# Masking the second batch's scores on TensorE inside the first layer, and moving two batches' global queries to the next first layer

## The chip, the cores and the metric

The kernel runs on one core of a Trainium2 chip. The metric is the time of one execution on the device, in microseconds (us). Lower is better. Most executions of one kernel agree within some 0.3%. A run more than 1.5% above the fastest of its kernel is called slow and is left out of every comparison. In a profile, PE is TensorE (matmuls), PEld its weight loads, DVE is VectorE, ACT is ScalarE, POOL is GpSimd and SP is SyncE, whose queue issues nearly all transfers. The granted clock is TensorE's clock as the profile records it, as a share of full speed.

## The reference

The program is an attention, followed by two dense layers with a gate between them. There are 8 batches of 8 heads with 512 local and 32 global tokens of width 64. A local query sees all global keys and the local keys within 32 positions. A global query sees everything.

```python
s_g   = scale * q_g @ concat(k_g, k_l).T;  out_g = softmax(s_g) @ concat(v_g, v_l)
s_ll  = where(abs(i - j) <= 32, scale * q_l @ k_l.T, -1e9)
s_lg  = scale * q_l @ k_g.T
out_l = softmax(concat(s_lg, s_ll)) @ concat(v_g, v_l)
x = concat(out_g, out_l) as (4608 tokens, 512)
h = x @ w_in                        # 512 x 2048
y = (h * clip(h + 3, 0, 6) / 6) @ w_out   # 2048 x 512
```

## The kernel before

The heads are worked in pairs. There are four pairs to a batch, so 32 in all, and pairs 0 to 3 are the first batch. A pair goes through these steps:

- load q, k and v, and cast them to fp16;
- transpose q and k (`emit_T` on TensorE, `emit_TD` by DMA from pair 8 on);
- score in two blocks of 128x512 for each head, with the exponential on ScalarE and the window mask;
- multiply with V and normalise (`emit_AV`), then transpose the output (`emit_X`).

The global queries have their own scores (`emit_SG`) and their own product with V (`emit_PG`). That product reads a V tile in which the last 63 columns of each head hold ones, so that the sums of the softmax come out of the same matmul. The texts below call these columns "the ones". The dense layers of a batch are cut into units: 16 of the first layer (`u1`, four 128x512 matmuls each) and 16 of the second (four each). `M(n)` issues the next n units that wait in a list. From the third batch on these units are woven between the attention steps of the next batch.

The mask is made in two ways. The first batch adds minus 30000 on TensorE, by an identity matmul that opens the group. All later batches multiply by 0 or 1 on VectorE:

```python
def emit_S(p, ch, pe_mask=False):
    ...
    if pe_mask:
        for e in range(2):
            nc.tensor.matmul(out=pss[e], lhsT=ident, rhs=mneg[:, ch], start=True, stop=False, ...)
    for w in range(NT): ...            # eight score matmuls of 128 columns
    for e in range(2):
        nc.scalar.activation(out=E[:, ch, e], in_=pss[e], func=EXP, scale=qk_scale)
    for e in range(0 if pe_mask else 2):
        nc.vector.tensor_tensor(out=E[:, ch, e], in0=E[:, ch, e], in1=mk[:, ch]..., op=mult)
```

`pin` fixes the program order of some engines. The GpSimd and SP queues are pinned everywhere, all five engines at the start, and only TensorE besides the queues in the second batch. The part at issue, after the first batch's attention:

```python
u1(HEAD)
nc.vector.tensor_scalar(out=mk..., in0=mneg, ...)       # 0/1 mask
for c in range(HEAD + 1, HEAD + 6):
    u1(c)
emit_G(1, 4, "kg")          # cast and transpose global keys of batches 2 to 4
u1(HEAD + 6)
emit_G(0, 4, "qg")          # the same for global queries
u1(HEAD + 7)
...
emit_SG(0) ... emit_PG(3)   # global queries of batch 1
pin(*ALL)
for p in range(NM, NPAIR):  # pairs 4 to 31
    load(p + 5); ...
    if p == 2 * NM - 1:     # the last pair of batch 2: first layer of batch 2 follows
        ...
    pin(*QUEUES, *((ET.PE,) if b == 1 else ()))
```

The softmax here doesn't subtract the row's maximum and nothing guards it: scores larger than these inputs give would overflow.

## Time and profile before

| | before |
|---|---|
| median time (beside the changed kernel) | 339.94 us, 339.4 to 341.44 in 4 runs |
| span of the profiled run | 337.2 us |
| TensorE busy, mean granted clock | 313.1 us (93%), 0.953 |
| VectorE, ScalarE, GpSimd busy | 229.0, 198.8, 133.1 us |

A high busy share of TensorE doesn't mean useful work at full speed. Matmuls at half clock also count as busy, so busy time has to be read together with the clock: from 57.1 to 71.9 us the clock was 0.50, and TensorE still counts as busy for 9.45 of 14.80 us. The prediction quotes the views by stage. One row of the costliest groups is needed besides (line, engine, operation, output and inputs, number, then busy us, mean ns of one, and idle time before them with what ended it):

```profile
L257 DVE TENSOR_TENSOR E<-E,mk 128x512 f16<-128x512 f16 x108 | 59.9, 586 | 22.0 <-ACT E L254 20.2
```

These are 108 of the mask multiplies. Four more are on another line, so there are 112: seven batches of 16.

### The profile page before, as it was taken

To read this page: it belongs to the slowest core of one execution; us is meant where nothing else is said; L and a number is where in the kernel's file an instruction comes from. 1 tells how busy PE (TensorE), PEld (TensorE's weight loads), DVE (VectorE), ACT (ScalarE), POOL (GpSimd) and SP (SyncE) were. 2 spreads that over 40 slices of the span, in tenths; PEclk is the share of its full clock that TensorE was granted. 3 is DMA by queue.
4 is the path that set the end of the run, shared out by engine and by line. 5 is a ranking of instruction groups with operands and counts; after the bars stand their busy time and mean duration, and the time that the engine had idled before them with its cause. 6 is when DMAs were issued, how large, how long until landed. Compare 5 with 4: busy or idle time off the path is not lost.

```text
span 337.2 us, 7418 instructions
## 1 busy us (share of the span) xinstructions
PE 313.1 (93%) x2784; PEld 165.2 (49%) x2784; DVE 229.0 (68%) x499; ACT 198.8 (59%) x394; POOL 133.1 (39%) x224
## 2 busy tenths in 40 slices
PE   6897794579999999999999999999999999999994
PEld 2453353444555555555555555555555555444571
DVE  7578688767946578847995689479945892473170
ACT  3588295637833459645974597458745881372260
POOL 7999999357203363326433633264230000000000
PEclk9699698569999999999999999999999999999999
DMA  8999999996099999769898997798943003101102
GB/s 215 316 362 271 331 361 209 187 200 126 2 171 193 204 204 175 144 129 217 167 149 167 206 178 134 130 231 172 136 124 99 18 16 80 62 0 33 71 24 62
DMA packets 139571, 52.92 MB, mean 157 GB/s; under 512 B 126992, under 2 KB 131088, under 8 KB 139536
## 3 DMA queue, kind: packets, MB, share of 16 engines
q1 hardware_dynamic: 137360, 52.19, 71.0%
q0 software_dynamic: 2176, 0.26, 1.2%
q8 instruction: 22, 0.36, 0.5%
q14 instruction: 13, 0.11, 0.1%
HBM read 35.13 MB, written 8.91 MB: 131 GB/s over the span
## 4 chain that ended last, share of the span: by engine, by line
PE 83%; DVE 5%; ACT 4%; POOL 3%; DMA 2%; issue 1%; POOLq 0%
PE po L397 35%; PE psH L381 33%; PE psS L250 4%; DVE gt L388 2%; PE pav L318 2%; PE pav L315 2%; DMA stg<-in_k_g_dram 2%; PE pg L338 2%; ACT vt L472 1%; PE psSG L292 1%; ACT t L386 1%; PE psS L269 1%; DVE xn L324 1%; PE psX L354 1%; DVE E L257 1%
## 5 line engine op out<-in xcount | busy, mean ns | idle before, releaser
L397 PE MATMUL po<-wout,gt 128*128 128x512 f16 x544 | 125.5, 379 | 0.0
L381 PE MATMUL psH<-xt,win 128*128 128x512 f16 x512 | 120.3, 385 | 0.5 <-DVE xt L358 0.5
L388 DVE SCALAR_TENSOR_TENSOR gt<-t,psH 128x512 f16<-128x512 f32 (+1 forms) x144 | 92.0, 654 | 27.5 <-ACT t L386 27.1
L386 ACT ACTIVATE t<-psH,half_col 128x512 f32<-128x512 f32 (+1 forms) x144 | 93.0, 669 | 26.7 <-PE psH L381 26.0
L254 ACT ACTIVATE E<-psS 128x512 f16<-128x512 f32 x108 | 55.6, 603 | 54.6 <-PE psS L250 54.6
L381 PEld LDWEIGHTS <-win 128*128 128x128 f16 x576 | 54.2, 99 | 55.1 <-issue 3.4
L397 PEld LDWEIGHTS <-gt 128*128 128x128 f16 x544 | 49.9, 98 | 54.3
L257 DVE TENSOR_TENSOR E<-E,mk 128x512 f16<-128x512 f16 x108 | 59.9, 586 | 22.0 <-ACT E L254 20.2
L238 POOL COPY qT<-qT 128x32 f16<-128x32 f16 x24 | 5.2, 216 | 119.0 <-DMA qT<-qn 93.4
L401 ACT COPY ot<-po 128x512 f32<-128x512 f32 x17 | 10.0, 586 | 29.4 <-PE po L397 29.4
L324 DVE TENSOR_TENSOR xn<-pav,rc 128x256 f16<-128x256 f32 x64 | 26.0, 420 | 1.3
L401 DVE COPY ot<-po 128x512 f32<-128x512 f32 x17 | 11.7, 691 | 19.4 <-PE po L397 19.4
L136 POOL CAST vt<-stg 128x512 f16<-128x512 f32 x32 | 21.5, 673 | 1.5 <-DMA stg<-in_v_l_dram 1.3
L315 PE MATMUL pav<-vt,E 128*128 128x65 f16 x256 | 21.2, 197 | 0.9 <-ACT E L254 0.9
L318 PE MATMUL pav<-vb,E 128*128 128x65 f16 x256 | 21.2, 198 | 0.0
L141 POOL COPY vb<-vt 64x512 f16<-64x512 f16 x32 | 20.1, 627 | 2.1
L323 DVE RECIPROCAL rc<-pav 128x4 f32<-128x4 f32 x64 | 10.1, 172 | 15.5 <-PE pav L318 15.4
L136 POOL CAST qn<-stg 128x512 f16<-128x512 f32 x31 | 20.5, 662 | 0.0
L315 PEld LDWEIGHTS <-E 128*128 128x128 f16 x256 | 18.9, 101 | 3.1
L318 PEld LDWEIGHTS <-E 128*128 128x128 f16 x256 | 17.9, 100 | 3.8 <-issue 1.0
L136 POOL CAST kn<-stg 128x512 f16<-128x512 f32 x31 | 19.4, 625 | 0.9
L250 PE MATMUL psS<-qT,kT 64*128 64x128 f16 x432 | 17.8, 224 | 1.5 <-DVE qT L222 1.5
(83 smaller groups left out, 261.8 us busy)
## 6 DMA issues: line engine op xcount, KB each, us to landing
stg<-in_k_l_dram SPq DMA_DIRECT2D x32, 256.0 KB, 3.8
stg<-in_q_l_dram SPq DMA_DIRECT2D x32, 256.0 KB, 4.2
stg<-in_v_l_dram SPq DMA_DIRECT2D x32, 256.0 KB, 4.7
out_dram<-ot SPq DMA_DIRECT2D x24, 256.0 KB, 2.3
stg<-in_moe_w_in_dram SPq DMA_DIRECT2D x16, 256.0 KB, 5.7
stg<-in_moe_w_out_dram SPq DMA_DIRECT2D x16, 256.0 KB, 5.7
out_dram<-ot SPq DMA_DIRECT2D x8, 192.0 KB, 2.2
out_dram<-ot SPq DMA_DIRECT2D x16, 64.0 KB, 1.8
```

Source lines behind the costliest of these rows:

```text
L136: eng.tensor_copy(out=o, in_=s[c + "f"])
L250: nc.tensor.matmul(out=pss[2 * ch + e][:, w * P:(w + 1) * P], lhsT=kT[r, c0:c0 + P], rhs=qT[r, w * P:(w + 1) * P])
L254: nc.scalar.activation(out=E[:, ch, e], in_=pss[2 * ch + e], func=EXP, scale=qk_scale)
L257: nc.vector.tensor_tensor(out=E[:, ch, e], in0=E[:, ch, e], in1=mk[:, ch].rearrange("p w c -> p (w c)"), op=mult)
L315: nc.tensor.matmul(out=o, lhsT=E[:, 0, e, w * P:(w + 1) * P], rhs=vt[:, w, h, 0:D + 1], start=True, stop=False, skip_group_check=True)
L318: nc.tensor.matmul(out=o, lhsT=E[:, 1, e, w * P:(w + 1) * P], rhs=vb[:, (w - 1) % NT, h, 0:D + 1], start=False, stop=True, skip_group_chec ...
L324: nc.vector.tensor_tensor(out=xn[:, 2 * w2:2 * w2 + 2].rearrange("p w (e d) -> p w e d", e=2), in0=pv[:, :, :, 0:D], in1=rc.to_broadcast([ ...
L381: nc.tensor.matmul(out=ps[:, 0:n], lhsT=w_in_t[m][:, c * P:(c + 1) * P], rhs=rhs(m), start=(m == 0), stop=(m == NM - 1), skip_group_check= ...
L386: nc.scalar.activation(out=t1[:, 0:n], in_=ps[:, 0:n], func=RELU, bias=half_col, scale=1.0 / 6.0)
L388: nc.vector.scalar_tensor_tensor(out=gts[c][:, 0:n], in0=t1[:, 0:n], scalar=1.0, in1=ps[:, 0:n], op0=amin, op1=mult)
L397: nc.tensor.matmul(out=po[t][:, 0:dm], lhsT=gts[c][:, t * P:(t + 1) * P], rhs=w_out_t[c // 4][:, c % 4], start=(c == 0), stop=(c == NC - 1))
L401: (nc.scalar.copy if t % 2 else nc.vector.tensor_copy)(out=ot, in_=po[t][:, 0:dm])
```

## The change

The intent is to give TensorE work to do while the second batch's attention waits for the other engines. The first layer of batch 1 is woven with that attention instead of running ahead of it. Batch 2's masks go to TensorE, where there is room, because VectorE would otherwise be too full. The global queries of batches 1 and 2 move into the first layer of batch 2. The order of all engines is now fixed up to the scores of pair 8. Besides this, pair 1 is loaded and cast earlier, the casts of global keys and queries are issued ahead of their transposes, and half of the fills of ones go from ScalarE to VectorE.

```diff
     load(0, "kq")
     load_g(0, 1, "kg")
+    load(1, "kq")
     load(0, "v")
-    for p in range(1, NM):
+    load(1, "v")
+    for p in range(2, NM):
         load(p, "kqv")
@@ first layer of batch 1, cut
-    for c in range(HEAD + 1, HEAD + 6):
-        u1(c)
-    emit_G(1, 4, "kg")
-    u1(HEAD + 6)
-    emit_G(0, 4, "qg")
+    u1(3)
+    u1(4)
+    cast_G(1, 4, "kg")
+    u1(5)
+    u1(6)
+    emit_G(1, 4, "kg")
+    ...
+    emit_T(5, True)
+    u1(9)
+    emit_S(4, 0)           # emit_S now always masks on TensorE
+    u1(10)
+    emit_S(4, 1)
+    ...                    # pairs 5 to 7 in the same way, up to u1(15)
+    emit_AV(7)
+    M(1)
+    emit_X(7)
+    M(2)
+    po_end = units.pop(0)
+    ...
+    emit_G(0, 4, "qg")
+    M(2)
+    po_end()               # first output tile of batch 1, and its stores
+    emit_SG(0)
+    ...
+    for p in range(NM):
+        emit_PG(p)
+    emit_XG(0)
+    feed(4)                # loads, casts, DMA transposes for later pairs
+    M(1)
+    emit_SG(4)
+    ...
+    for u in range(NT):
+        ones_v(1, u, nc.vector)     # was on ScalarE, in the first stage
+    M(2)
+    feed(5)
+    for p in range(NM, 2 * NM):
+        emit_PG(p)
+    emit_XG(1)
+    ...
+    pin(*ALL)
+    emit_S2(2 * NM)
@@ in the loop, now from pair 8 on
-        if p == 5:
+        if p == 9:
             load_g(4, B, "kg"); load_g(4, B, "qg")
```

More of the change, by code (lines that the diff above doesn't have):

```diff
@@ L145, in vglob, with vgsum @@
                         in_=vg[rg, b].unsqueeze(1).to_broadcast([Sg, NT, H, D]))
-        if b:
-            eng.tensor_copy(out=vgs[b % NV][rg, :, 0:D], in_=vg[rg, b])
+    def vgsum(b, eng):
+        eng.tensor_copy(out=vgs[b % NV][rg, :, 0:D], in_=vg[rg, b])
     def load_vg(b):
@@ L181, in load_g, with cast_G @@
         gst[b0, nm] = t
+    def cast_G(b0, b1, nm):
+        n = wrk.tile([P, 4 * P], FP16, tag="gn", name=nm + "n", bufs=2)
+        nb = b1 - b0
+        nc.vector.tensor_copy(out=n[:, 0:nb * P], in_=gst[b0, nm][:, 0:nb * P])
+        gst[b0, nm, "n"] = n
     def emit_G(b0, b1, nm):
         nb = b1 - b0
-        n = wrk.tile([P, 4 * P], FP16, tag="gn", name=nm + "n", bufs=2)
-        nc.vector.tensor_copy(out=n[:, 0:nb * P], in_=gst[b0, nm][:, 0:nb * P])
+        if (b0, nm, "n") not in gst:
+            cast_G(b0, b1, nm)
+        n = gst[b0, nm, "n"]
         psT = ps_tile("psGT", FP16)
@@ L258, in emit_S2, with emit_Sm, emit_Ss @@
                                         in1=mk[:, ch].rearrange("p w c -> p (w c)"), op=mult)
-    def emit_S(p, ch, pe_mask=False):
+    def emit_Sm(p, ch):
+        pss = st[p]["ps", ch] = [ps_tile(f"psS{e}") for e in range(2)]
+        for e in range(2):
+            nc.tensor.matmul(out=pss[e], lhsT=ident, rhs=mneg[:, ch], start=True, stop=False,
+                             skip_group_check=True)
+    def emit_Ss(p, ch):
         s = st[p]
-        qT, kT = s["qT"], s["kT"]
-        if ch == 0:
+        qT, kT, pss = s["qT"], s["kT"], s["ps", ch]
+        if "E" not in s:
             s["E"] = wrk.tile([P, 2, 2, Sl], FP16, tag="E", name="E", bufs=3)
-        E = s["E"]
-        pss = [ps_tile(f"psS{e}") for e in range(2)]
-        if pe_mask:
-            for e in range(2):
-                nc.tensor.matmul(out=pss[e], lhsT=ident, rhs=mneg[:, ch], start=True, stop=False,
-                                 skip_group_check=True)
         for w in range(NT):
@@ L275, in emit_S @@
                 nc.tensor.matmul(out=pss[e][:, w * P:(w + 1) * P], lhsT=kT[r, c0:c0 + P],
-                                 rhs=qT[r, w * P:(w + 1) * P], start=not pe_mask, stop=True,
+                                 rhs=qT[r, w * P:(w + 1) * P], start=False, stop=True,
                                  skip_group_check=True)
         for e in range(2):
-            nc.scalar.activation(out=E[:, ch, e], in_=pss[e], func=EXP, scale=qk_scale)
-        for e in range(0 if pe_mask else 2):
-            nc.vector.tensor_tensor(out=E[:, ch, e], in0=E[:, ch, e],
-                                    in1=mk[:, ch].rearrange("p w c -> p (w c)"), op=mult)
+            nc.scalar.activation(out=s["E"][:, ch, e], in_=pss[e], func=EXP, scale=qk_scale)
+    def emit_S(p, ch):
+        emit_Sm(p, ch)
+        emit_Ss(p, ch)
     def emit_SG(p):
@@ L468, in fill_v, with ones_v @@
         eng.memset(vts[i][:, :, :, D:D + 1], 1.0)
-    def ones_v(i):
-        for u in range(NT):
-            nc.scalar.copy(out=vts[i][:, u, :, D + 1:P],
-                           in_=ones.unsqueeze(2).to_broadcast([P, H, D - 1]))
+    def ones_v(i, u, eng=None):
+        o = vts[i][:, u, :, D + 1:P]
+        if eng is None:
+            nc.scalar.copy(out=o, in_=ones.unsqueeze(2).to_broadcast([P, H, D - 1]))
+        else:
+            eng.memset(o, 1.0)
     def fill_vg(i, eng):
@@ L491 @@
     fill_v(1, nc.gpsimd)
+    cast(1, "kq", nc.gpsimd)
     first(0, "v")
+    first(1, "v")
+    for p in range(2, NM):
+        first(p)
     load_vg(1)
+    for i in range(NC):
+        cast_w("in", i, nc.gpsimd)
+    units += moe_units(lambda mm: xts[0][mm], Sl, local_dests(0), early=True)
+    u1 = units.pop(0)
     emit_T(0)
     nc.scalar.memzero(qgz)
-    units += moe_units(lambda mm: xts[0][mm], Sl, local_dests(0), early=True)
-    u1 = units.pop(0)
-    for p in range(1, NM):
-        first(p)
-    for i in range(NC):
-        cast_w("in", i, nc.gpsimd)
-    emit_S(0, 0, True)
+    emit_Sm(0, 0)
+    emit_Sm(0, 1)
+    emit_Ss(0, 0)
     emit_G(0, 1, "kg")
@@ L506 @@
     vglob(0, nc.vector)
-    emit_S(0, 1, True)
-    emit_S(1, 0, True)
+    emit_Ss(0, 1)
+    emit_S(1, 0)
     emit_T(2)
-    emit_S(1, 1, True)
+    emit_S(1, 1)
     emit_AV(0)
     emit_T(3, True)
-    emit_S(2, 0, True)
+    emit_S(2, 0)
     emit_X(0)
-    emit_S(2, 1, True)
+    emit_S(2, 1)
     emit_AV(1)
-    emit_S(3, 0, True)
+    emit_S(3, 0)
     emit_X(1)
-    emit_S(3, 1, True)
-    ones_v(0)
-    ones_v(1)
+    emit_S(3, 1)
+    for u in range(NT):
+        ones_v(0, u)
     emit_AV(2)
@@ L532 @@
         u1(c, range(3, 4))
-    fill_vg(0, nc.gpsimd)
-    fill_vg(1, nc.gpsimd)
     for p in range(NM, 2 * NM):
         first(p)
+    fill_vg(0, nc.gpsimd)
+    vgsum(0, nc.gpsimd)
+    fill_vg(1, nc.gpsimd)
+    vgsum(1, nc.gpsimd)
     load_vg(2)
@@ L539 @@
         cast_w("out", i, nc.gpsimd)
-    u1(HEAD)
-    nc.vector.tensor_scalar(out=mk.rearrange("p c w q -> p c (w q)"), in0=mneg, scalar1=-1.0,
-                            scalar2=1.0, op0=is_ge, op1=mult)
+    u1(3)
[4 more added lines that the diff above has]
+    emit_G(1, 4, "kg")
+    u1(7)
+    kglob(1, nc.vector)
+    vglob(1, nc.vector)
+    emit_T(4)
+    u1(8)
+    emit_T(5, True)
[3 more added lines that the diff above has]
+    emit_S(4, 1)
+    emit_T(6)
+    u1(11)
+    emit_S(5, 0)
+    emit_AV(4)
+    emit_S(5, 1)
+    u1(12)
+    emit_T(7, True)
+    emit_X(4)
+    emit_S(6, 0)
+    emit_AV(5)
+    u1(13)
+    emit_S(6, 1)
+    emit_X(5)
+    emit_S(7, 0)
+    emit_AV(6)
+    u1(14)
+    emit_S(7, 1)
+    cast_G(0, 4, "qg")
+    emit_X(6)
+    u1(15)
+    emit_AV(7)
[3 more added lines that the diff above has]
+    po_end = units.pop(0)
+    u2 = moe_units(lambda mm: xts[1][mm], Sl, local_dests(1))
+    units[:0] = u2[0:NC]
+    units += u2[NC:]
+    M(1)
     for t in Egs:
         nc.vector.memset(t[:, NT], 0.0)
-    for c in range(HEAD + 1, HEAD + 6):
-        u1(c)
-    emit_G(1, 4, "kg")
-    u1(HEAD + 6)
     emit_G(0, 4, "qg")
-    u1(HEAD + 7)
-    kglob(1, nc.vector)
-    vglob(1, nc.vector)
-    nc.vector.tensor_copy(out=vgs[0][rg, :, 0:D], in_=vg[rg, 0])
-    units[:0] = [lambda c=c: u1(c) for c in range(HEAD + 8, NC)]
-    M(1)
+    M(2)
+    po_end()
     emit_SG(0)
@@ L558, with feed @@
     M(1)
-    emit_T(4)
     emit_SG(2)
     emit_SG(3)
-    M(1)
-    emit_S(4, 0)
-    emit_T(5)
+    M(2)
+    nc.vector.tensor_scalar(out=mk.rearrange("p c w q -> p c (w q)"), in0=mneg, scalar1=-1.0,
+                            scalar2=1.0, op0=is_ge, op1=mult)
     for p in range(NM):
         emit_PG(p)
-    M(1)
-    emit_S(4, 1)
-    emit_SG(4)
     emit_XG(0)
-    M(1)
-    pin(*ALL)
-    for p in range(NM, NPAIR):
+    def feed(p):
         b, m = divmod(p, NM)
@@ L582 @@
                 vglob(b + 1, nc.gpsimd)
+                vgsum(b + 1, nc.gpsimd)
             cast(p + 4, "kqv", nc.gpsimd)
@@ L586 @@
             kglob(b + 1, nc.gpsimd)
-        if p == 5:
-            load_g(4, B, "kg")
-            load_g(4, B, "qg")
-        if p == 10:
-            emit_G(4, B, "kg")
-            emit_G(4, B, "qg")
-        n = (0, 0, 0, 0) if b == 1 else (1, 1, 1, 2) if p == 2 * NM else (1, 2, 2, 3)
         if m == 2 and b + 2 < B:
@@ L597 @@
             emit_TD(p + 3)
-        if p + 2 < 2 * NM:
-            emit_T(p + 2)
-        M(n[0])
-        if p == 2 * NM - 1:
-            emit_AV(p)
-            emit_PG(p)
-            emit_X(p)
-            emit_XG(b)
-            u2 = moe_units(lambda mm, b=b: xts[b][mm], Sl, local_dests(b))
-            units[:0] = u2[0:NC]
-            units += u2[NC:]
-            M(NC - 3)
-            emit_S2(p + 1)
-            M(2)
-            emit_SG(p + 1)
-            M(1)
-        else:
-            if p + 1 < NPAIR:
-                emit_S2(p + 1)
-            M(n[1])
-            if p + 1 < NPAIR:
-                emit_SG(p + 1)
-            M(n[2])
-            emit_AV(p)
-            emit_PG(p)
-            M(n[3])
-            emit_X(p)
-            if m == NM - 1:
-                emit_XG(b)
-                units += moe_units(lambda mm, b=b: xts[b][mm], Sl, local_dests(b))
-        pin(*QUEUES, *((ET.PE,) if b == 1 else ()))
+    feed(4)
+    M(1)
+    emit_SG(4)
+    emit_SG(5)
+    M(1)
+    emit_SG(6)
+    emit_SG(7)
+    for u in range(NT):
+        ones_v(1, u, nc.vector)
+    M(2)
+    feed(5)
+    for p in range(NM, 2 * NM):
+        emit_PG(p)
+    emit_XG(1)
+    M(2)
+    feed(6)
+    feed(7)
+    M(1)
+    pin(*ALL)
+    emit_S2(2 * NM)
+    M(2)
+    emit_SG(2 * NM)
+    M(1)
+    for p in range(2 * NM, NPAIR):
+        b, m = divmod(p, NM)
+        feed(p)
+        if p == 9:
+            load_g(4, B, "kg")
+            load_g(4, B, "qg")
+        if p == 12:
+            emit_G(4, B, "kg")
+            emit_G(4, B, "qg")
+        n = (1, 1, 1, 2) if p == 2 * NM else (1, 2, 2, 3)
+        M(n[0])
+        if p + 1 < NPAIR:
+            emit_S2(p + 1)
+        M(n[1])
+        if p + 1 < NPAIR:
+            emit_SG(p + 1)
+        M(n[2])
+        emit_AV(p)
+        emit_PG(p)
+        M(n[3])
+        emit_X(p)
+        if m == NM - 1:
+            emit_XG(b)
+            units += moe_units(lambda mm, b=b: xts[b][mm], Sl, local_dests(b))
+        pin(*QUEUES)
     M(len(units))
```

## The prediction

> **What bounds the kernel now.** I read the 40-slice picture first, because one number for the span mixes stages. Its TensorE rows show two regimes:
>
> ```profile
> PE   6897794579999999999999999999999999999994
> POOL 7999999357203363326433633264230000000000
> PEclk9699698569999999999999999999999999999999
> DMA  8999999996099999769898997798943003101102
> ```
>
> A slice is 8.4 us. From the tenth slice to the last but one TensorE is full at full clock: 250 us in which only removing TensorE work helps. Before that it has holes and a lowered clock, while GpSimd and the DMA are near full. Next I cut the head where its stages change (columns: stretch and length, busy us and instructions of PE, PEld, DVE, ACT, POOL, then granted clock, DMA share, GB/s):
>
> ```profile
> 0.00:26.10 26.10, 21.17 (x211) 10.64 (x212) 17.89 (x51) 15.99 (x28) 22.50 (x43) 0.87 1.01 297
> 26.10:41.00 14.90, 10.93 (x46) 4.63 (x46) 10.65 (x27) 7.57 (x13) 13.91 (x23) 0.82 1.12 296
> 41.00:71.90 30.90, 20.34 (x314) 14.79 (x313) 25.14 (x57) 19.13 (x47) 22.80 (x36) 0.72 1.09 249
> 71.90:87.30 15.40, 15.40 (x88) 7.03 (x87) 11.89 (x20) 11.72 (x20) 10.50 (x18) 0.96 0.65 123
> 87.30:291.10 203.80, 203.80 (x1908) 106.34 (x1907) 143.59 (x312) 124.21 (x253) 63.39 (x108) 1.00 0.75 144
> ```
>
> Busy time overstates overlapping matmuls, so I count work in full-clock durations taken from back-to-back runs in the timeline: a 128x512 matmul 0.216 us (64 in 13.81); transposing q and k of a pair 0.45; one half of a pair's scores 0.33; two mask matmuls 0.53; a pair's AV 0.49; its output transpose 0.23; its global scores 0.15, their product with V 0.25.
> 0 to 26.1 (attention of the first batch): 4x0.45 + 8x0.53 + 8x0.33 + 4x0.49 + 4x0.23 + 9x0.216 = 13.6; lost 12.5.
> 26.1 to 41.0 (39 first-layer matmuls, two global transposes): 8.8; lost 6.1.
> 41.0 to 71.9 (the rest of that layer, all global queries of two batches, second batch's attention): 3.5+1.8+0.7+1.7+1.2+2.0+2.0+0.9 = 13.7; lost 17.2.
> So 35.8 us are lost to idling or the lower clock before 71.9, and about 0.6 just after.
>
> Who causes it is in the waits (us in total, times, longest) of the third stretch, and in the chain that ended last:
>
> ```profile
> PE psX L354 <- DVE xn L324: 6.9, 7, 2.4
> PE psS L250 <- DVE qT L222: 1.5, 1, 1.5
> ...
> 33.70 0.28 DVE kgn L186
> ...
> 36.67 0.53 DVE qgn L186
> 37.20 0.05 issue
> 37.25 0.61 PE psGT L189 x4
> 37.86 3.43 PE psH L381 x8
> ...
> 58.29 5.57 DMA stg<-in_k_g_dram
> 63.85 0.02 issue
> 63.88 0.43 DVE kgn L186
> 64.31 0.09 DVE qT L222
> ```
>
> At 34 and 37 TensorE stands about 2 us each for a cast of global keys or queries queued behind VectorE work; then eight matmuls take 0.43 each, half clock. From 52 on, each pair is a bare chain of scores, exponential, mask multiply, AV, normalise, transpose, with no other matmul to fill it. At 58 to 64 VectorE's unpinned order put a cast of a later load before a small copy that the scores need.
>
> **What the Trainium skill says.** "Perfetto Trace Analysis", Optimization Strategy, advises interleaving regimes whose contended engine differs: exactly this change; the 71.9 to 291 stretch, interleaved, loses almost nothing. "TensorE: Matmul & The Clock Gate", part 1, says that an idle window of about 3.4 us halves the clock and a busy one restores it; the trace agrees (clock 0.50 from 57.1 to 71.9; 0.43 against 0.216 above). "PSUM — Partial Sum Buffer", The four PSUM rules, says a seed goes through an identity matmul that opens the group; the first batch's masks do just that. "GPSIMD Engine Reference", Specifications, says that its SBUF interface is shared with VectorE and two-input instructions contend; the mask multiply takes 0.39 at best, but two took 1.80 at 53 us beside a busy GpSimd.
>
> **The change part by part.**
> Masks of batch 2: 16 VectorE multiplies (0.586 mean, 9.4 us) go; 16 mask matmuls come, 8x0.53 = 4.2 us of TensorE at full clock. The pairs are also scored in halves, 3x0.11 = 0.3. VectorE was on the path there; TensorE was idle, so this pays in the head only.
>
> First stage: pair 1 is loaded and cast earlier and two masks are issued before the first scores. TensorE waited 1.27 for pair 1's k; but pairs 2 and 3 still come from the same GpSimd sequence, whose length is unchanged. Half of ScalarE's eight 0.5 us fills of ones leave (its first ReLU was late by some 0.4). I end this stage at 25.0 instead of 26.1.
>
> Second stage (the first layer woven with attention of batch 2): 55 matmuls 11.9, transposes 1.8, global keys 0.2, scores with masks 4x(1.06+0.66) = 6.9, AV 2.0, output transposes 0.9: 23.7 of TensorE. VectorE: 13 products at 0.61, key, query and wrap copies about 4.8, AV 4.4, outputs 1.7, globals 2.5: 21.3. ScalarE: 13x0.59 + 16x0.5 + 1.2 = 16.9. TensorE is longest, barely. Waits I add: pair 4 needs casts that GpSimd starts after w_in (ended at 27.2) and a load that lands about 29 to 30; pair 5's q was issued at 29.5 and lands about 33.5. Together 2.5; one reclocking after it 1; the last pairs' VectorE latencies 1.5. So 28.7, ending at 53.7. The output-weight casts should end near 55.5 (GpSimd has 40 for pairs 4 to 7, then fills 3.0, two sums 1.5, an issue 0.6, sixteen casts 10.5), so the second-layer units sit just behind them: units one to three need casts up to 52.9, the fourth comes four units later.
>
> Third stage (global queries of both batches woven into the next first layer): 16 first-layer and 4 second-layer units at 0.864 = 17.3, global scores 9x0.15, products 8x0.25, transposes 0.3, next scores 0.55: 21.5. ScalarE has 16x0.59 + 8x0.6 + 1.7 + 2.6 = 18.5, VectorE about 17. I add 2 for waits. It ends at 77.2, at the state that the kernel before reaches at 87.3, with 4 second-layer units (3.5) already done.
>
> The rest: 337.2 - 87.3 = 249.9, less 3.5 = 246.4. At each later batch boundary three left-over second-layer units no longer separate the last transpose from the new first layer. In the present trace at 119 the copy of that transpose ends at 119.64, and three matmuls of the new unit that don't need it cover 0.65 from 119.18, so I charge nothing.
>
> Sum: 77.2 + 246.4 = 323.6 of span; the median time is 339.97 against a span of 337.2, so add 2.8: 326.4. By losses: 36.4 before, 11.4 + 5 + 2 = 18.4 after, a gain of 18; less 4.5 for added masks and halves leaves 13.5.
>
> **Rivals.** (a) GpSimd becomes the bound. The V sum and V tile of batch 3 overwrite buffers that batch 1's global products read, and those are now late. From their end GpSimd needs the sum 0.8, a k and q cast 1.3; then two DMA transposes (about 2.7 of issue), 2.7 to land, a wrap copy 0.3: 7.0 with its queue of casts. TensorE reaches the scores of pair 8 after seven units and small work, 7.65. The slack is 0.65, so a slow transpose (4 us to land) costs 1 to 3: 328 to 330. (b) The DMA share of 1.1 binds and the head can't be shortened, as loads of pairs 5 to 7 come when they come: then stage two ends near 58 and the time is about 331. Against: the saturated work needed by pair 8 is smaller than before, since the 0.5 MB of later global loads and one pair move behind it. (c) The pinned order stands in line at each missed wait, and each gap drops the clock for a window; three episodes at 1.7 make 331 to 332. (d) All weaves well, losses of 2.5 and 1 in stages two and three and an earlier first stage: 321.
>
> **Range and chances.** The gain in waits is plain in the profile, and the remaining 250 us can't move much, so the sign is fairly safe. The low end takes (d) and a bit more, 317; the high end two of the rivals together, 336. A 2% gain needs under 333.2: chance 0.83; within 2%: 0.14; slower: 0.03, for a hidden stall on casts or loads in the pinned part.
>
> **What would show it.** In the changed profile the 2 us stops at the global casts should be gone, and the global load off the chain; stage two should end (last AV of pair 7) near 53.7 and hold 16 more mask matmuls of 0.216; the mask multiplies should number 96 instead of 112; the scores of pair 8 should start near 74 with little wait; the slices from the tenth on should be full at clock 1.00, with no new wait at the batch boundaries. It is wrong if TensorE's idle in stage two exceeds 8 us, if GpSimd's wrap copy releases the scores of pair 8 late by over 3 us, or if the tail after pair 8's state isn't near 246.

## The result, and the profile after

The changed kernel takes 331.07 us (median of 4 runs, 330.8 to 335.9, of which the 335.9 is a slow run). The kernel before took 339.94 us on the same chip. A ratio here is the mean time of one kernel's fast runs over the mean of the other's fast runs of the same rounds, so it isn't quite the ratio of the quoted medians. It is 0.973 (95% interval 0.969 to 0.977), which is faster by over 2%. The prediction's working came to 326.4, a gain of 13.5 us, in a range of 317 to 336. The gain measured is 8.9.

The 40-slice picture of the changed kernel (a slice is 8.2 us):

```profile
PE   7698898979999999999999999999999999999994
POOL 6895899175574365346521633363330000000000
PEclk9789999998999999999999999999999999999999
DMA  7999999199999998999799979797763002101202
```

The holes of the fourth to eighth slices have mostly closed, and the clock is at 90% or more there. Two weak places are left: slices two and three, where the clock shows a 7 and an 8, and slices nine and ten, where TensorE shows a 7 and then the clock an 8. The stretches show the same in numbers (stretch and length, then busy us of PE, PEld, DVE, ACT, POOL with instruction counts, granted clock, DMA share, GB/s):

```profile
27.40:56.10 28.70, 26.04 (x255) 13.37 (x255) 23.65 (x53) 19.91 (x34) 24.30 (x41) 1.00 1.06 290
56.10:69.70 13.60, 13.60 (x136) 7.27 (x134) 7.83 (x21) 9.71 (x24) 6.10 (x9) 1.00 0.48 99
69.70:77.90 8.20, 5.96 (x57) 2.78 (x58) 5.33 (x11) 4.50 (x11) 4.68 (x9) 0.79 1.04 179
```

The first row is the woven stage: TensorE is busy for 26.04 of 28.70 us, at full clock. The kernel before spent its stretch from 41.0 to 71.9 at a clock of 0.72. The next stage starts just as well, with 13.6 us without a hole. Then come 8.2 us with 2.2 us of idling and a lowered clock. The chain that ended last shows what happens there (start, us, what):

```profile
69.64 0.69 DVE gt L397
...
70.39 0.48 DVE vt L486
...
71.98 0.49 DVE vt L486
...
73.61 4.29 PE psH L390 x12
77.89 0.55 PE psS L258 x16
```

TensorE's wait for it (in total, times, longest):

```profile
PE pg L347 <- DVE vt L486: 2.2, 4, 1.2
```

L486 is the fill of ones, four times 0.48 us on VectorE. Batch 2's global products read these columns, so TensorE stands from the end of its first-layer matmuls at 69.70 until the last fill at 72.46, with three single matmuls in between. The clock then drops: twelve first-layer matmuls take 4.29 us instead of 2.6 (12 x 0.216). The scores of pair 8 start at 77.89, where the prediction had about 74.

A second thing is going on behind this one. SP's own waits from 50 to 80 us (in total, times, longest), and two rows of GpSimd's timeline, whose brackets give the idle time before and what ended it:

```profile
SPq L412 <- DVE ot L410: 9.2, 1, 9.2
```

```profile
65.72 0.61 POOL L148 COPY vgs<-vg 32x512 f16<-32x512 f16 x1 [7.25 <-PE pg L349]
...
75.47 0.21 POOL L246 COPY qT<-qT 128x32 f16<-128x32 f16 x1 [3.33 <-DMA qT<-qn]
```

SP stood 9.2 us, to 63.33, before the store of batch 1's first finished output tile. The loads of pairs 9 and 10 stand behind that store in the same queue. They went out from 64.25 to 69.66, and the first DMA transpose of pair 8 only at 69.76. GpSimd stood 7.25 us until batch 1's global products had released the buffer of the V sum (`vgs`, the tile that the last matmul of each global product reads), and the casts for pairs 8 and 9 stand behind that sum. So the wrap copy (L246, a copy of 32 columns of the transposed queries), the last thing that pair 8's scores need, came at 75.47. It didn't hold TensorE in this run, because TensorE was held for longer by the ones and the half clock after them.

The row of mask multiplies, which answers to the one shown of before:

```profile
L265 DVE TENSOR_TENSOR E<-E,mk 128x512 f16<-128x512 f16 x96 | 49.9, 546 | 27.7 <-ACT E L262 25.5
```

There are 96, which is 16 fewer than before. Each is also a little shorter, 546 ns against 586.

### The profile page after: what moved, and what is told of

Its sections match the earlier page's. It is cut to its first block, busy times and chain, and to the rows that moved or that the text cites. A ratio compares the mean times of both kernels' runs of the same rounds, so it can differ in the third digit from the quotient of the medians.

```text
span 329.2 us, 7431 instructions
## 1 busy us (share of the span) xinstructions
PE 312.9 (95%) x2800; PEld 163.2 (50%) x2800; DVE 217.0 (66%) x487; ACT 197.2 (60%) x388; POOL 133.2 (40%) x226
## 4 chain that ended last, share of the span: by engine, by line
PE 78%; DMA 6%; POOL 4%; DVE 4%; ACT 3%; issue 2%; SPq 1%; POOLq 0%; ACTq 0%
PE po L406 35%; PE psH L390 30%; PE psS L258 4%; PE pav L324 2%; PE pav L327 2%; DMA stg<-in_moe_w_in_dram 2%; DMA stg<-in_v_l_dram 2%; DMA stg<-in_q_l_dram 2%; ACT t L395 2%; PE pg L347 2%; DVE gt L397 1%; DMA xt<-xn 1%; POOL win L170 1%; POOL vt L136 1%; PE psSG L301 1%
## 5 line engine op out<-in xcount | busy, mean ns | idle before, releaser
L390 PE MATMUL psH<-xt,win 128*128 128x512 f16 x512 | 121.9, 383 | 1.5 <-DVE gt L397 0.6
L397 DVE SCALAR_TENSOR_TENSOR gt<-t,psH 128x512 f16<-128x512 f32 (+1 forms) x144 | 90.7, 651 | 28.9 <-ACT t L395 28.3
L395 ACT ACTIVATE t<-psH,half_col 128x512 f32<-128x512 f32 (+1 forms) x144 | 92.4, 669 | 28.5 <-PE psH L390 27.8
L390 PEld LDWEIGHTS <-win 128*128 128x128 f16 x576 | 53.2, 98 | 52.8 <-issue 4.4
L265 DVE TENSOR_TENSOR E<-E,mk 128x512 f16<-128x512 f16 x96 | 49.9, 546 | 27.7 <-ACT E L262 25.5
L262 ACT ACTIVATE E<-psS 128x512 f16<-128x512 f32 x96 | 49.4, 603 | 9.7 <-PE psS L258 9.7
L246 POOL COPY qT<-qT 128x32 f16<-128x32 f16 x24 | 5.2, 218 | 102.3 <-DMA qT<-qn 78.5
L333 DVE TENSOR_TENSOR xn<-pav,rc 128x256 f16<-128x256 f32 x64 | 26.1, 420 | 1.4
L287 ACT ACTIVATE E<-psS 128x512 f16<-128x512 f32 x32 | 17.4, 595 | 5.5 <-PE psS L283 4.9
L324 PE MATMUL pav<-vt,E 128*128 128x65 f16 x256 | 20.3, 194 | 0.0
L327 PE MATMUL pav<-vb,E 128*128 128x65 f16 x256 | 20.3, 195 | 0.0
L324 PEld LDWEIGHTS <-E 128*128 128x128 f16 x256 | 18.0, 98 | 3.7 <-issue 0.2
L327 PEld LDWEIGHTS <-E 128*128 128x128 f16 x256 | 17.2, 98 | 3.0
L258 PEld LDWEIGHTS <-kT 64*128 64x128 f16 x384 | 10.8, 94 | 10.3 <-issue 8.6
```

Source lines behind the costliest of these rows:

```text
L258: nc.tensor.matmul(out=pss[2 * ch + e][:, w * P:(w + 1) * P], lhsT=kT[r, c0:c0 + P], rhs=qT[r, w * P:(w + 1) * P])
L262: nc.scalar.activation(out=E[:, ch, e], in_=pss[2 * ch + e], func=EXP, scale=qk_scale)
L324: nc.tensor.matmul(out=o, lhsT=E[:, 0, e, w * P:(w + 1) * P], rhs=vt[:, w, h, 0:D + 1], start=True, stop=False, skip_group_check=True)
L327: nc.tensor.matmul(out=o, lhsT=E[:, 1, e, w * P:(w + 1) * P], rhs=vb[:, (w - 1) % NT, h, 0:D + 1], start=False, stop=True, skip_group_chec ...
L333: nc.vector.tensor_tensor(out=xn[:, 2 * w2:2 * w2 + 2].rearrange("p w (e d) -> p w e d", e=2), in0=pv[:, :, :, 0:D], in1=rc.to_broadcast([ ...
L390: nc.tensor.matmul(out=ps[:, 0:n], lhsT=w_in_t[m][:, c * P:(c + 1) * P], rhs=rhs(m), start=(m == 0), stop=(m == NM - 1), skip_group_check= ...
```

## The experiments

The theory after reading the two traces was this. The weaving and the TensorE masks work as meant. The missing 4.7 us are lost in the stage before pair 8, first to the fill of ones ("wall 1") and then, if that is removed, to the late intake of pairs 8 to 10 ("wall 2"). The rivals were that the late first stage costs the time, that the saving is in a part other than the weaving, or that the fill alone explains the miss. All kernels below give correct results. Each was run four times, beside the kernel before on the same chip (339.57 to 339.84 us in all three batches of runs). The three batches ran on three chips, so differences between runs of different batches, and from the change, lean on this agreement and on the ratios.

**e1: the second V tile's ones on GpSimd, after its casts of output weights.**

```diff
     for i in range(NC):
         cast_w("out", i, nc.gpsimd)
+    for u in range(NT):
+        ones_v(1, u, nc.gpsimd)
...
-    for u in range(NT):
-        ones_v(1, u, nc.vector)
```

> The changed kernel, with the four fills of ones of the second V tile taken from VectorE (four of 0.48 us, at 70.4 to 72.5, for which TensorE stood from 69.7 to 72.5) to GpSimd, right after the output-weight casts, where GpSimd later waits 7.25 us anyway. Theory (the fill held TensorE for about 2.8 us and then cost 1.7 us more at half clock): time 331.1 - 4.5 = 326.6, and granted clock 1.00 from 56 to 81. Rival (the scores of pair 8 can't start before GpSimd's wrap copy of its queries, which came at 75.5 to 75.7, while they started at 77.8): the gain stops at about 2.2, so 328.9, and TensorE shows a new wait for that copy. If the fills weren't on the path at all: 331.

The result is 332.46 us (331.79 to 333.26), ratio 0.978, so not faster than the change as it stands, and far from both the theory (326.6) and the rival (328.9). Waits of TensorE, over the whole run:

```profile
PE psS L258 <- POOL qT L246: 3.6, 3, 1.7
PE psH L390 <- DMA xt<-xn: 1.6, 1, 1.6
```

The stop for the ones is gone, and no half clock follows in this stage. TensorE now waits three times for the wrap copy: 1.69 us before pair 8's scores (75.89), then 0.73 and 1.20 for pairs 9 and 10. The scores of pair 10 start at 88.08. In the changed kernel they start at 87.95. Wall 2 has taken the whole gain. The second line is a wait at the next batch boundary, where the changed kernel waits 0.3.

**e2: batch 2's masks on VectorE again, everything else as changed.**

```diff
-        for e in range(2):                    # emit_Sm: identity matmul with the mask
+        for e in range(2 if p < NM else 0):
...
+        for e in range(2 if p >= NM else 0):  # after the exponential
+            nc.vector.tensor_tensor(out=E[:, ch, e], in0=E[:, ch, e], in1=mk[:, ch]..., op=mult)
...                                           # and the 0/1 mask made earlier, after u1(3)
```

> The changed kernel, with the second batch's masks back on VectorE as 16 multiplies (0.4 to 0.6 us each) and no mask matmuls for it; weaving and global queries stay moved. Theory (in the woven stage VectorE, busy 23.65 of 28.7 us, has no room for another 7 to 9 us, while TensorE has the 4.2 us of mask matmuls nearly free): the stage gets 3 to 5 us longer, time 334 to 336. Rival (TensorE is the longest engine there, so 4.2 us less of it is a gain): 327 to 329. If waits for loads set the stage's end: 331.

The result is 337.16 us (336.89 to 338.71), ratio 0.992. The woven stage of this kernel, over the same stretch:

```profile
27.40:56.10 28.70, 21.02 (x206) 10.94 (x205) 27.38 (x61) 16.92 (x31) 24.58 (x39) 0.92 1.02 288
```

VectorE is at 27.38 of 28.70 us, so it has become the bound. TensorE falls from 26.04 to 21.02 and its clock to 0.92. The two second-layer units that follow the stage start at 62.1 us instead of 55.9. Of the 8.9 us that the change gains, 6 vanish when the masks stay on VectorE, more than the theory's 3 to 5. The weaving needs the masks on TensorE. What these masks would give without the weaving was not run, so that half is not shown.

**e3: load and GpSimd order at the start as before.**

```diff
-    load(1, "kq")
     load(0, "v")
-    load(1, "v")
-    for p in range(2, NM):
+    for p in range(1, NM):
         load(p, "kqv")
...
-    cast(1, "kq", nc.gpsimd)
     first(0, "v")
-    first(1, "v")
...                       # load_vg(1) and the casts of pairs 1 to 3 follow, as before
```

> The changed kernel, with the order of the first loads and of GpSimd's first casts as in the kernel before (pair 0's V first, then pairs 1 to 3; the load of the second V of the globals early). TensorE's order stays. Theory (the new order made GpSimd wait for pair 1's k, and everything on GpSimd came 1.3 us later: input-weight casts from 18.0 instead of 16.7, the first stage ending at 27.4 instead of 26.1): time 331.1 - 1.3 = 329.8, input-weight casts from 16.7. Rival (the first stage is longer because TensorE now waits 2.1 us for pair 2's k and drops its clock, which the early masks bring about whatever the load order): no gain, 331, first stage still ends after 27.

The result is 331.02 us (329.69 to 331.86), ratio 0.974, the same as the change. The first stage did end sooner, at 24.78 against 27.41, at full clock (how much of this is the order and how much the clock is worked out in the part on the prediction):

```profile
0.00:24.80 24.80, 19.27 (x211) 9.86 (x212) 17.34 (x51) 14.51 (x25) 21.04 (x40) 1.00 1.02 299
```

Only half of these 2.6 us are left at the end of this run, whose span is 327.9 against 329.2. TensorE still stands 2.2 us for the ones. The scores of pair 8 start 2.6 sooner (75.25). Before those of pair 10 TensorE waits 0.56 for the wrap copy, which leaves 2.0, and at the batch boundary it waits 0.95 for a DMA-transposed tile instead of 0.26. The profiled run is also the fastest of the four (329.69), and the other three show no gain over the change. What an earlier first stage gives is partly taken by waits further on, and the rest is not above the scatter of 2.2 us.

**e4: the kernel before, with only the early casts and the later global loads.**

```diff
-    for c in range(HEAD + 1, HEAD + 6):
+    for c in range(HEAD + 1, HEAD + 4):
         u1(c)
+    cast_G(1, 4, "kg")
+    u1(HEAD + 4)
+    cast_G(0, 4, "qg")
+    u1(HEAD + 5)
     emit_G(1, 4, "kg")
...
-        if p == 5:
+        if p == 9:
             load_g(4, B, "kg")
```

> The kernel before with one part of the change alone: the casts of global keys and queries issued one to two units before their transposes, and the later global loads moved from pairs 5 and 10 to pairs 9 and 12. Theory (two stops of 2 us at 34 to 37 us, 1.7 us of half clock after them, and 1.5 us behind the stray cast at 64 were all on the path): 340 - 6 = 334, which would be two thirds of the change's gain. Rival (the second batch's attention then waits for GpSimd's casts and loads, which don't come sooner): 337 to 338. If nothing of it was on the path: 340.

The result is 338.8 us (336.33 to 339.3), ratio 0.995: nearly nothing. The two stretches that the prediction quotes of before, now in this kernel:

```profile
26.10:41.00 14.90, 12.21 (x82) 5.73 (x81) 13.43 (x31) 11.66 (x24) 13.91 (x22) 1.00 1.07 283
41.00:71.90 30.90, 18.41 (x280) 13.57 (x281) 24.73 (x53) 15.39 (x37) 25.56 (x40) 0.69 1.10 255
```

In the first stretch TensorE gets on better (12.21 busy at clock 1.00, against 10.93 at 0.82). In the second it stands more: 18.41 at 0.69, against 20.34 at 0.72. TensorE got to the bare chain of attention sooner and waited there for the output normalisation, 8.5 us against 6.9. The stops at the casts were worth almost nothing alone.

**e5: the intake of batch 3 ahead.** Pairs 9 and 10 are loaded right after pair 8, before any store. GpSimd casts q and k of pairs 8 and 9 before the sum of V, and their DMA transposes are issued earlier.

```diff
     load(2 * NM)
+    load(2 * NM + 1)
+    load(2 * NM + 2)
...
+        if p == NM:
+            vglob(2, nc.gpsimd)
+            cast(8, "kq", nc.gpsimd)
+            emit_TD(8)
+            cast(9, "kq", nc.gpsimd)
+            kglob(2, nc.gpsimd)
+            vgsum(2, nc.gpsimd)
+            cast(8, "v", nc.gpsimd)
+            vshift(8, nc.gpsimd)
+            return
...                       # the same for pair 9 at p == NM + 1
```

> The changed kernel with only the intake of batch 3 loosened: the loads of pairs 9 and 10 are issued before the first output stores instead of behind them, and GpSimd casts k and q of pairs 8 and 9 and hands them to the DMA transposes before the copies (sum of V, V tiles) that must wait for the first batch's global products. The ones stay on VectorE. Theory (the ones and the intake are two walls at nearly the same time, and either alone is enough to hold TensorE until 77.8 and 88.0): time 331, plus or minus 1; but the wrap copy of pair 8 comes by 71 instead of 75.5. Rival (the intake alone sets the pace): 327 to 328.

The result is 330.07 us (329.39 to 330.32), ratio 0.971. The wrap copy of pair 8 comes at 68.84 instead of 75.47, and TensorE still stands 2.2 us for the ones. Wall 2 alone is also worth little.

**e6: e1 and e5 together.** The edits are those two.

> Both at once: the ones on GpSimd (which alone gave 332.5) and the loosened intake. Theory (two walls, one behind the other): scores of pair 8 near 73.5 to 74 instead of 77.8, no wait for the wrap copies, 331.1 - 4 = 327. Rival (the early loads crowd the output-weight loads, or the casts come no sooner): 330 to 332.

The result is 325.62 us (325.46 to 325.76), ratio 0.958. The stage from 56.1 to 81.3, where the changed kernel has TensorE at 22.96 us and a clock of 0.93:

```profile
56.10:81.30 25.20, 24.90 (x280) 13.91 (x279) 17.78 (x42) 21.39 (x50) 16.31 (x27) 1.00 0.97 178
```

TensorE is full at full clock, with 280 matmuls in the stretch against 222. The scores of pair 8 start at 72.58. The third stage, with the same 222 matmuls, runs from 55.02 to 76.29, that is 21.3 us instead of 25.2. Against the changed kernel, removing wall 1 alone gave nothing, removing wall 2 alone gave 1.0 us, and removing both gave 5.5. This settles the two walls: each hides the other.

**e7: e6 with the start order of e3.**

> As the run before, with the first loads and casts also in the order of the kernel before (which alone ended the first stage at 24.8 instead of 27.4 and yet gave only 331.0 in the median). Theory (its 2 to 2.6 us were swallowed by the same wall): now they come through, 327 - 2.3 = 324.7. Rival (loads of pairs 4 to 7 or output-weight casts pace the second stage, so the earlier start is waited away): 326 to 327.

The result is 325.23 us (324.93 to 326.15), ratio 0.958. Its interval (0.9553 to 0.9605) covers the ratio of e6, so the start order still adds nothing clear. The theory took its 2.3 us from e3, against a run of the change whose start was at half clock. In e6 the start was at full clock, and there was little left to gain: the first stage ends at 24.46 us in e7 and at 25.17 in e6, and the profiled spans are 323.3 and 323.7. TensorE now waits a little more for the casts of the next pairs (3.2 us in all for k, 1.4 for q). It is the fastest version by its median, 14.3 us below the kernel before and 5.8 below the change.

**e8: the first batch's global queries back in the woven stage.**

```diff
+    cast_G(0, 4, "qg")
     u1(9)
     emit_S(4, 0)
+    emit_G(0, 4, "qg")
     u1(10)
     emit_S(4, 1)
+    emit_SG(0)
+    emit_SG(1)
...
+    for p in range(NM):
+        emit_PG(p)
+    emit_XG(0)
     emit_X(5)
...                       # and the same calls taken out of the next first layer
```

> The changed kernel with one move undone: the global queries of the first batch are scored and multiplied in the woven second stage again, those of the second batch stay in the next first layer. Theory (the move made the first batch's global products late, which holds the buffers that GpSimd needs for batch 3): GpSimd's 7.25 us wait shrinks to under 2, but loads 9 and 10 stay behind the stores, so the wrap copy of pair 8 comes 2 to 4 us sooner; the ones remain: time 329 to 331. Rival (ScalarE and VectorE are too full in the second stage to take 4 more exponentials pairs and 1.7 us of copies, so that stage grows by 2 us or more): 331 to 333.

The result is 333.21 us (332.66 to 333.88), ratio 0.981, so some 2 us worse than the change: moving these queries out of the woven stage was worth about that. The rival's reason holds. The woven stage runs from 25.68 to 59.02 us, 33.3 instead of 28.7. GpSimd's wait for the buffer is gone, but the wrap copy comes later than in the change, at 77.09, where sooner had been expected:

```profile
69.89 0.61 POOL L136 CAST kn<-stg 128x512 f16<-128x512 f32 x1 [9.49 <-DMA stg<-in_k_l_dram]
```

GpSimd now waits 9.49 us for pair 9's k. That load still stands behind the first store, which went out at 65.41 here, 2.1 us later than in the change, after the longer stage. So of the two halves of wall 2 the order of SP's queue holds first.

**e9: only TensorE and the queues pinned; VectorE and ScalarE free.**

```diff
-    pin(*ALL)
+    pin(*QUEUES, ET.PE)
```

> The changed kernel with the fixed order reduced: up to batch 3 TensorE, GpSimd and the load queue keep the program's order, VectorE and ScalarE are left to the compiler's scheduling, as in the second batch of the kernel before. Theory (the walls are the ones on VectorE, the loads behind the stores and the held buffers; the two engines' order matters only where a stray instruction waits, as the cast at 64 us in the kernel before): 331, within 1. Rival (fixing these two engines carries a good part of the gain): 334 or more. Third way (the free order puts the ones earlier): 328 to 330.

The result is 333.79 us (331.79 to 336.62), ratio 0.985 with an interval of 0.979 to 0.991. The runs scatter more than in any other kernel, so its distance to the change isn't measured well. The trace of its fastest run shows what freedom did to VectorE's order:

```profile
6.17 2.08 DVE L486 MEMSET vt<- 128x504 f16 x4
...
9.77 0.09 DVE L497 MEMSET mneg<- 128x32 f16 x1
```

The ones that stood in the way at 70 us are now filled at 6 us, where they stand ahead of the last pieces of the mask. TensorE waits 3.7 us for the mask. The first stage ends at 30.69 instead of 27.41. Freedom on VectorE removes wall 1 and builds another at the start, and TensorE still waits 3.1 us for the wrap copies.

**e10: e7 with pair 4's transpose one unit later.**

```diff
-    emit_T(4)
     u1(8)
-    emit_T(5, True)
+    emit_T(4)
     u1(9)
     emit_S(4, 0)
+    emit_T(5, True)
     u1(10)
```

> The best so far (ones, intake and start as in the run of all three, 325.2) with the second stage's first units shifted: one first-layer unit before the transposes of pair 4, and the first scores of pair 4 before the transposes of pair 5, so that TensorE has work while GpSimd casts pairs 4 and 5, for which it waited 0.8 and 1.5 us. Theory (those waits are now on the path): 325.2 - 1.5 = 323.7. Rival (the waits only move, to later casts or to VectorE's output transposes): 325 to 325.5.

The result is 326.21 us (325.87 to 326.53), ratio 0.960, no gain. The wait for the casts falls from 3.2 to 1.5 us, but 1.9 us of waiting for a copy of queries, without which the scores cannot begin, come in.

**e11 and e12: the two halves of the intake, each with the ones on GpSimd.** e11 has e5's early loads only, e12 has e5's order of casts only, with the loads still behind the store and pair 8's DMA transposes issued where the change has them.

> One half of the loosened intake: ones on GpSimd, and the loads of pairs 9 and 10 issued before the first output stores; GpSimd's order as in the changed kernel, so the casts still wait behind the sum of V for the first batch's products. Theory (the load queue's order is the larger half: the DMA transposes of pair 8 stood behind loads 9 and 10, which stood behind stores that wait for the first finished output at 63 us): wrap copy of pair 8 by 72 instead of 75.5, time 326 to 327.5, against 332.5 for the ones alone. Rival (held buffers are the larger half): 330 to 332.

> The other half: ones on GpSimd, and GpSimd casts k and q of pairs 8 and 9 before the copies that wait for the first batch's products; loads 9 and 10 stay behind the stores. Theory (the load queue's order is what holds): casts of pair 9 now wait for its load, in front of the copies, so pair 8's transposes are not sooner: 331 to 333. Rival (held buffers are the larger half): 326 to 328.

e11 gives 327.55 us (326.45 to 328.2), ratio 0.964. e12 gives 330.35 (329.64 to 331.62), ratio 0.973, a little better than expected. TensorE's waits from 56 to 92 us for the wrap copy, first e11, then e12:

```profile
PE psS L258 <- POOL qT L246: 0.4, 1, 0.4
```

```profile
PE psS L258 <- POOL qT L246: 3.4, 3, 1.7
```

The early loads cut this wait from 3.6 us in e1 to 0.4 and are worth 4.9 us against e1. The casts alone leave it at 3.4 and are worth 2.1; where these come from wasn't traced. The order of the loads against the store is the larger half.

## Why the prediction was right or wrong, point by point

**The sign and the mechanism were right.** The stops of 1.95 and 2.02 us at the global casts are down to 0.3, the later global load is off the chain, and the mask multiplies are 96. Experiment e2 confirms that the masks had to leave VectorE for the weaving to pay in full. But e4 shows that the stops at the casts, which the prediction named first, were worth almost nothing alone. So the gain came with the filled attention chain: taking the masks back costs 6.1 us (e2), taking the first batch's global queries back 2.1 (e8), and taking the start order back nothing clear (e3). These are not shares that add up, and the weaving was never run or removed by itself.

**The sum, term by term.** The differences in the profiled run:

| term | predicted | measured | difference |
|---|---|---|---|
| first stage ends | 25.0 | 27.41 | +2.4 |
| woven stage (without one second-layer unit, 0.86, counted later) | 28.7 | 28.69 - 0.86 = 27.8 | -0.9 |
| third stage, to the state of pair 8 | 23.5 | 81.29 - 56.09 + 0.86 = 26.1 | +2.6 |
| the rest of the span | 246.4 | 329.2 - 81.3 = 247.9 | +1.5 |
| median time less span | 2.8 | 331.07 - 329.2 = 1.9 | -0.9 |
| sum | 326.4 | 331.1 | +4.7 |

The prediction's own sums were redone. The work before 26.1 adds up to 13.5 and not 13.6, the work from 41.0 to 13.8 and not 13.7, which cancels. The terms of rival (a) add up to 7.8 and not 7.0 (see below).

**First stage: the term had no drop of the clock.** The prediction let it end 1.1 us earlier than before. It ended 1.3 later. GpSimd now meets pair 1's k before it has landed: it idled 2.03 us for it, then 0.20 and 0.35 for q and V, and its casts of input weights began at 18.00 instead of 16.72. So the length of GpSimd's sequence is unchanged in its work, but not in its waiting. TensorE waited 2.14 us for pair 2's k, and from about 12.4 to 19.1 us it ran at half clock. That half clock is most of the miss. e6 has the same start order and ran its start at full clock, and the stage ended at 25.17, next to the 25.0 predicted. The runs with the old order, all at full clock, ended it at 24.78, 24.46 and 24.40 (e3, e7, e10). So the order itself costs 0.4 to 0.8 us here. The half clock comes in some executions of this start and not in others: from the change and from e1, e2, e5, e6, e8, e11 and e12, one profile of each, the stage ended anywhere from 25.17 to 27.41. In the time of the change it hardly shows: its three fast runs had mean clocks of 0.984, 0.993 and 0.987, and spans of 329.2, 329.0 and 329.3 us. And mending the term alone brings no difference that four runs resolve, with the walls (e3) or without (e7).

**Woven stage: right, even a little too careful.** The prediction had added 5 us of waits. The waits of TensorE in the trace come to about 3, with no drop of the clock. Its mark for the end, the last AV of pair 7, came at 53.0 to 53.7, where it had said 53.7, although the stage began 2.4 late.

**Third stage: this is the step that failed.** The prediction says "I add 2 for waits" and gives VectorE "about 17" of busy time. It counted the fills of ones as work that leaves ScalarE's first stage, but didn't ask where on VectorE they would stand or who waits for them. In a pinned order they stand just before the products that read them. They cost 2.2 us of recorded waiting, and 1.7 more in the half clock that follows (4.29 less 2.6). In e6, with both walls removed, this stage takes 76.29 - 55.02 + 0.86 = 22.1 us, less than the 23.5 predicted.

**Rival (a) was right in kind and too small.** It saw that GpSimd's V sum would wait for batch 1's products, and gave the way from there to the wrap copy 7.0 us. The terms that it lists add up to 7.8, which is already more than the 7.65 that it allows. From 65.72 to the end of the copy at 75.68 it took 10.0. It missed two things. SP was still issuing the loads that had stood behind the first store, so the transposes, whose casts ended at 67.76, started only at 69.76. And their issue took 3.05 and 1.20 us instead of 2.7 in all.

**Rival (c) came true, and the prediction listed it apart from (a).** It said that the pinned order stands in line at each missed wait, that the clock then drops, and that the time is 331 to 332. Wall 1 is such a wait, there were two stretches at half clock (12.4 to 19.1 and 73.8 to 77.2), and the time is 331.07. For its high end the prediction set two rivals side by side, at 336. But these two lie one behind the other, so that the larger hides the smaller, and it takes both removals to see the gain (e1, e5, e6). With both removed the terms of the table are 25.2, 29.0, 22.1, 247.4 and 1.9, in sum 325.6, each within 1.4 of the prediction's. Rival (b), with stage two ending near 58 behind its loads, didn't show: it ended at 56.1, with a second-layer unit in it.

**The batch boundaries: "I charge nothing" was wrong by a little.** The prediction looked only at the output transpose that TensorE makes, the last of a batch. The other three go by DMA. At 113.0 a first-layer unit waits 0.3 us for one of these, and at 187 a unit waits 0.6 for VectorE. Idle time from 81.3 to 285.1 is 203.80 - 202.94 = 0.86. The remaining 0.6 of the 1.5 isn't traced to a wait and stays open. In e1 and e8 the DMA wait at the boundary grew to 1.6 and 1.1 us.

## What to carry to other kernels

When work is moved to another engine in a fixed order, ask what stands in front of it there and who waits for it: 2 us of fills, moved from ScalarE's first stage to VectorE, held TensorE for 2.2 us and lowered its clock. Follow the transfers as strictly as the compute, since a load issued after a store on one queue waits for whatever the store waits for (9.2 us here). If removing one stop gains nothing, look at what was ready just behind it before calling the stop harmless, and remove both.

## What the Trainium skill lacked or had wrong

- "TensorE: Matmul & The Clock Gate", part 1, gives about 3.4 us for the window that halves the clock, but not how much work inside it still counts as idle. Here the clock was halved from about 73.8 to 77.2 us (worked out from its readings of 0.65, 0.50, 0.50 and 0.65 in the four microseconds from 73.5). The longest stretch around the stop was only 69.70 to 72.5, and three short matmuls ran inside it. In the first stage the clock fell about 1.3 us into a stop that began at 11.09. In e1 a stop of 1.69 us didn't lower the clock. The prediction's "the trace agrees" holds for the half rate alone: the stops before the half clock at 37 us were 1.95 and 2.02 us.
- "DMA: Bandwidth & Descriptors", Issuing engines are not separate DMA queues, says that issuing from several engines only saves time on the sequencer, "usually small relative to the DMA itself". That counts the time of issuing. The section doesn't speak of a transfer that waits for its data and holds those issued after it on the same engine: here SP stood 9.2 us before one store, and moving six loads ahead of that store gained 4.9 us (e11 against e1). No run issued these loads from another engine.
- No page gives the time of a fill with a constant on GpSimd: for 128x504 elements of fp16 it took 0.52 us (e1), against 0.48 for the same fill on VectorE.
